# Attention and gated FFN on one core: scores in stages of eight blocks that cross units, values in one stage per unit, eight PSUM banks shared out anew, three load slots

## The chip, the core and the metric

The kernel runs on one core of a Trainium2 chip. The metric is the device time in microseconds (us) of one execution; of the kernel before, three runs gave a median of 1071.33 us (1071.3 to 1072.25).

## What is computed

Windowed causal attention with a linear bias over 8 batches of 8 heads (576 positions, head size 64), and then a gated FFN on all 4608 tokens (model width 512, hidden width 1536). All in fp32; q, k and the gate's weights are drawn several times wider than usual.

```python
scores = q @ k.transpose(0, 1, 3, 2) / sqrt(64)
mask = (rel >= 0) & (rel < 128)                       # rel = query position - key position
scores = where(mask, scores - slope[h] * abs(rel), -1e9)
attn = softmax(scores)                                # sum + 1e-9 in the denominator
x = (attn @ v) laid out as (4608, 512)
gate = 1 / (1 + exp(-(x @ w_gate)))
out = (gate * (x @ w_val)) @ w_out
```

## The kernel before, in words

**Attention** is worked in 32 *units*: one batch and a pair of heads each. The two heads' 1152 tokens are cut into 9 *blocks* of 128 queries. A block's queries see its own 128 keys and the 128 before them, so its scores are one matmul of 64 contraction rows into 256 columns (the first block of a unit: 128). Even blocks lie on the lower 64 rows of TensorE's array and odd ones on the upper 64, and two such matmuls run side by side. In the kernel before a unit's blocks go in three *score stages* of 3, 4 and 2 blocks (`group`, line 339), into the two banks `sp`; for the first four units every other stage goes into two of the FFN's banks instead. VectorE (DVE) then merges each bank's two halves (line 350), adds the bias and takes the row minimum (line 356, "the reduction"); ScalarE (ACT) takes the exponential with its sum (line 360); DVE makes the reciprocal; DVE or ACT scales the row (lines 368 and 369). TensorE transposes the group's blocks into the bank `tp` (line 373), ACT or DVE copies them out, and GpSimd spreads them into `pt` with the triangle masks (line 384). The *values* (line 409) are matmuls of 128 rows into 64 columns, one head on the lower and one on the upper half of the array's columns, side by side too. A unit has two value stages: output positions 0 to 320 and 320 to 576. The result is copied to `xt` and sent to DRAM (`xs`).

**The FFN** keeps fp32 accuracy with three fp32r products a matmul (high and low parts). Its first third of the hidden width (`w1`, tiles of 512 tokens, nine of them) runs among the attention: per tile 4 gate and 4 value projections of 12 matmuls each (line 454), each in one PSUM bank, and 4 output projections of 12 (line 492), 144 matmuls in all. After a value projection DVE multiplies by the gate in the bank (line 470), ACT casts the high part (line 173) and DVE subtracts for the low part (line 182); only then is the bank free. The other two thirds (`w2`, lines 584 to 615) run behind, with a scheme of seven products; they need the attention's SBUF, which is given back when the last unit is done, and weights that are split on DVE and ACT from then on.

**PSUM** has eight banks of 128 x 512: before, four (`mm0` to `mm3`) for the FFN, two for the scores, one for the transposes, one for the values.

**What sets the order.** Every piece of work is an `Op` with an engine, a cost and keys that it reads and writes. `Graph.order` is a list scheduler: it takes the op that can start first, ties by its due time `want` (FFN matmuls on TensorE come last), and the engines then get their instructions in that fixed order. One `add` is one piece: a whole score stage, a whole value stage, three FFN matmuls. Outside the first units every attention piece on TensorE is planned to start 1 us (`SLACK`) after its inputs. All DMAs go out on SP's queue.

Of the kernel before, what the change touches and what calls it, by code (L numbers as in the profile page):

```python
# [150 lines left out]
def attention_gated_ffn(ctx: ExitStack, tc: tile.TileContext, qd, kd, vd, wg, wv, wo, out):  # L151
# [88 lines left out]
    raws, mms, banks = [0], [0], [4]  # L240
# [64 lines left out]
    def load(u):  # L305
        want = u.when(-len(GROUPS))
        cuts = (0, 3, NBLK) if u.n == 0 else (0, NBLK)
        for h, (b0, b1) in enumerate(zip(cuts, cuts[1:])):
            sl, q0, q1 = slice(b0 * P, b1 * P), (b0 + 1) // 2, (b1 + 1) // 2
            keys = range(b0, b1)  # L310
            move(lambda sl=sl: kraw(u)[:, sl], lambda sl=sl: kd[u.b, u.p, :, sl], [], [("kr", u.s, i) for i in keys], want, 64 * (b1 - b0))
            move(lambda q0=q0, q1=q1: qraw(u)[:, q0:q1], lambda q0=q0, q1=q1: qd[u.b, u.p, :, q0:q1], [],
                 [("qr", u.s, i) for i in range(2 * q0, 2 * q1)], want, 64 * (q1 - q0))
        move(lambda: vraw(u), lambda: vd[u.b, u.p], [], [("vr", u.s)], want, 288)

    count = [0]

    def group(u, k):
        m = count[0]
        count[0] += 1  # L320
        blks = GROUPS[k]
        n = len(blks)
        want = u.when(k)
        slack = 0.0 if u.n < HEAD else SLACK
        early = u.n < EARLY and m % 2
        banks = [mm[r].rearrange("p (a q) -> p a q", a=2) for r in range(2)] if early else sp
        kbank = [("mm", r) if early else ("sp", r) for r in range(2)]
        kst, kpb, kb = ("st", m % 4), ("pb", m % 3), ("both", m % 2)
        st = lambda: T(att, f"st{m % 4}", [P, 12], F32)
        pb = lambda: T(att, f"pb{m % 3}", [P, 4, P], F32)  # L330
        both = lambda: T(att, f"both{m % 2}", [P, 4, P], F32)
        spot = {i: (i % 2, sum(j % 2 == i % 2 for j in blks[:a])) for a, i in enumerate(blks)}

        def scores():
            for i in blks:
                r, a = spot[i]
                lo = P if i == 0 else 0
                rows = slice(r * D, r * D + D)
                nc.tensor.matmul(banks[r][:, a, lo:], qraw(u)[rows, i // 2], kraw(u)[rows, (i - 1) * P + lo:(i + 1) * P],  # L339
                                 start=True, stop=True)  # L340
# [5 lines left out]
        for r in used:
            a = [spot[i][1] for i in blks if i % 2 == r and i]
            if a:
                a0, a1 = a[0], a[-1] + 1
                g.add("DVE", dve_cost((a1 - a0) * P, psum=True), lambda r=r, a0=a0, a1=a1: nc.vector.copy_predicated(  # L350
                    banks[r][:, a0:a1, P:], before[:, a0:a1], banks[r][:, a0:a1, 0:P]), ["before"], [kbank[r]], want)
            for e, i in enumerate(blks):
                if i % 2 == r:
                    mid = NBLK // 2
                    w = 0 if i == 0 else 1 if i < mid else min(4, i - mid + 2)
                    g.add("DVE", 0.21, lambda e=e, i=i, w=w: nc.vector.tensor_tensor_reduce(  # L356
                        pb()[:, e], banks[i % 2][:, spot[i][1], P:], relm[u.p][:, w], op0=ALU.add, op1=ALU.min,
                        scale=-0.125, scalar=3.0e38, accum_out=st()[:, e:e + 1]), [kbank[r]], [(kpb, e), (kst, e)], want)
# [370 lines left out]
```

## Time and profile before

| | |
|---|---|
| median of 3 runs | 1071.33 us (1071.3 to 1072.25) |
| profiled execution | 1071.71 us, span 1070.0 us, granted clock 0.997 |
| TensorE busy | 1059.2 us, 99% of the span |
| DVE, ACT, GpSimd busy | 694.1, 549.3 and 110.8 us |
| score matmuls (L339), as recorded | 576 records, 91 us |
| value matmuls (L409), as recorded | 832 records, 74.1 us |

[...] Recorded matmul durations overlap, so what TensorE needs for a piece is read from the distance between starts, not from the sum of the durations. The profiled execution is 1.71 us longer than its span and 0.38 us longer than the median.

### The profile page before, as it was taken

What the parts mean: (1) busy time and instruction counts of PE and PEld (TensorE: products, weight loads), DVE (VectorE), ACT (ScalarE), POOL (GpSimd) and SP (SyncE); (2) the same over time, 40 slices, a digit from 0 to 9 for tenths busy, and PEclk for the clock granted to TensorE, in tenths of its full rate; (3) what the DMA queues carried; (4) which work ended last, traced back from release to release, by engine and by line L of the source; (5) the groups of instructions that cost most, each with busy time, mean ns of one, the idle gap of its engine ahead of it and who ended that gap; (6) DMA issues with size and microseconds to landing.
All of it is one profiled execution on the core that took longest, in us unless ns stands there. A gap on an engine that the chain in (4) does not pass through costs nothing.

```text
span 1070.0 us, 17032 instructions
## 1 busy us (share of the span) xinstructions
PE 1059.2 (99%) x5918; PEld 894.3 (84%) x5918; DVE 694.1 (65%) x1958; ACT 549.3 (51%) x1503; POOL 110.8 (10%) x207
## 2 busy tenths in 40 slices
PE   8899999999999999999999999999999999999998
PEld 6577677777777778888999899998989989899997
DVE  7896656665655638863565675746999465675743
ACT  7997776576667745432443352433755234251431
POOL 2333222222222210000000000000000000000000
PEclk9899999999999999999999999999999999999999
DMA  7667546545364415441222415134353532415122
GB/s 244 224 216 237 157 149 188 167 147 161 115 194 167 129 62 188 157 132 65 99 87 91 138 40 177 51 127 137 101 165 108 161 98 80 146 32 177 51 69 98
DMA packets 74726, 142.66 MB, mean 133 GB/s; under 512 B 7312, under 2 KB 30224, under 8 KB 74640
## 3 DMA queue, kind: packets, MB, share of 16 engines
q1 hardware_dynamic: 74640, 141.58, 40.7%
q8 instruction: 46, 0.75, 0.3%
q14 instruction: 40, 0.33, 0.1%
HBM read 103.81 MB, written 37.75 MB: 132 GB/s over the span
## 4 chain that ended last, share of the span: by engine, by line
PE 95%; ACT 2%; DVE 1%; DMA 1%; issue 0%; SPq 0%; ACTq 0%; DVEq 0%
PE mm L584 33%; PE mm L492 27%; PE mm L454 19%; PE sp L339 7%; PE avp L409 6%; PE tp L373 3%; ACT pb L360 1%; DMA xr<-xs 1%; ACT pb L368 0%; DVE xlo L182 0%; DMA qr<-in_q_dram 0%; ACT both L173 0%; DVE pb L356 0%; DVE mm L350 0%; PE mm L339 0%
## 5 line engine op out<-in xcount | busy, mean ns | idle before, releaser
L584 PE MATMUL mm<-xc,w2s 128*128 128x384 f32 x2016 | 354.9, 335 | 0.0
L584 PEld LDWEIGHTS mm<-xc,w2s 128*128 128x128 f32 x2016 | 351.2, 188 | 2.3 <-ACT a L173 0.3
L492 PE MATMUL mm<-w2o,hh 128*128 128x512 f32 x576 | 177.7, 390 | 0.0
L360 ACT ACTIVATE pb<-pb,st 128x128 f32<-128x128 f32 x288 | 113.2, 396 | 42.6 <-DVE st L356 42.4
L384 POOL TENSOR_SCALAR_AFFINE_SELECT pt<-both 128x384 f32<-128x384 f32 (+2 forms) x192 | 98.9, 540 | 276.3 <-ACT both L173 220.5
L492 PEld LDWEIGHTS mm<-w2o,hh 128*128 128x128 f32 x576 | 107.8, 188 | 21.3
L492 PE MATMUL mm<-w2o,hl 128*128 128x512 f32 x288 | 112.4, 390 | 0.0
L595 ACT ACTIVATE sg<-mm 128x384 f32<-128x384 f32 x96 | 47.4, 494 | 115.5 <-PE mm L584 76.2
L173 ACT COPY a<-mm 128x384 f32<-128x384 f32 x48 | 23.1, 481 | 148.1 <-PE mm L584 145.2
L454 PE MATMUL mm<-xhi,w1g 128*128 128x512 f32 x288 | 93.7, 407 | 0.4 <-DVE st L356 0.4
L454 PE MATMUL mm<-xhi,w1v 128*128 128x512 f32 x288 | 93.1, 404 | 0.0
L492 PE MATMUL mm<-w1o,hh 128*128 128x512 f32 x288 | 93.1, 404 | 0.0
L350 DVE COPY_PREDICATED sp<-before,sp 128x128 f32<-128x128 int32 (+1 forms) x180 | 52.8, 333 | 53.0 <-PE sp L339 52.4
L339 PE MATMUL sp<-kr,qr 64*128 64x128 f32 (+1 forms) x540 | 84.8, 406 | 1.4 <-DMA qr<-in_q_dram 0.8
L409 PEld LDWEIGHTS avp<-pt,vr 128*64 128x64 f32 x832 | 58.4, 137 | 25.6 <-issue 12.0
L591 DVE TENSOR_TENSOR mm<-mm,a 128x384 f32<-128x384 f32 x48 | 27.0, 563 | 72.9 <-PE mm L584 72.9
L409 PE MATMUL avp<-pt,vr 128*64 128x64 f32 (+3 forms) x832 | 74.1, 310 | 0.0
L368 ACT ACTIVATE pb<-pb,st 128x128 f32<-128x128 f32 x169 | 60.5, 398 | 19.3 <-DVE st L365 18.2
L339 PEld LDWEIGHTS sp<-kr,qr 64*128 64x128 f32 x540 | 46.5, 189 | 26.3 <-issue 13.8
L356 DVE CUSTOM_DVE_ANT_0 pb<-sp,relm 128x128 f32<-128x128 f32 x270 | 64.1, 283 | 0.1
L497 DVE SCALAR_TENSOR_TENSOR ob<-mm,pi 128x512 f32<-128x512 f32 x72 | 48.3, 684 | 23.7 <-PE mm L492 14.2
L492 PEld LDWEIGHTS mm<-w1o,hh 128*128 128x128 f32 x288 | 51.0, 188 | 14.9 <-issue 6.5
(109 smaller groups left out, 1516.7 us busy)
## 6 DMA issues: line engine op xcount, KB each, us to landing
part<-ob SPq DMA_DIRECT2D x72, 256.0 KB, 3.1
pi<-part SPq DMA_DIRECT2D x72, 256.0 KB, 3.3
kr<-in_k_dram SPq DMA_DIRECT2D x31, 576.0 KB, 4.4
xr<-xs SPq DMA_DIRECT2D x18, 768.0 KB, 5.5
qr<-in_q_dram SPq DMA_DIRECT2D x31, 320.0 KB, 4.9
vr<-in_v_dram SPq DMA_DIRECT2D x32, 288.0 KB, 3.5
xs<-xt SPq DMA_DIRECT2D x32, 288.0 KB, 3.7
out_dram<-ob SPq DMA_DIRECT2D x36, 256.0 KB, 2.1
```

The lines of the kernel that those rows point to most:

```text
L339: nc.tensor.matmul(banks[r][:, a, lo:], qraw(u)[rows, i // 2], kraw(u)[rows, (i - 1) * P + lo:(i + 1) * P], start=True, stop=True)
L350: g.add("DVE", dve_cost((a1 - a0) * P, psum=True), lambda r=r, a0=a0, a1=a1: nc.vector.copy_predicated(banks[r][:, a0:a1, P:], before[:, a ...
L356: g.add("DVE", 0.21, lambda e=e, i=i, w=w: nc.vector.tensor_tensor_reduce(pb()[:, e], banks[i % 2][:, spot[i][1], P:], relm[u.p][:, w], op ...
L360: g.add("ACT", 0.39, lambda e=e: nc.scalar.activation(pb()[:, e], pb()[:, e], AF.Exp, bias=st()[:, e:e + 1], scale=-1.0, accum_out=st()[:, ...
L368: g.add("ACT", 0.3, lambda args=args: nc.scalar.mul(*args()), [(kst, 8)], [(kpb, e)], want, ways=[("DVE", 0.16, True, lambda args=args: nc ...
L384: nc.gpsimd.affine_select(pt(u)[:, f0:f0 + 2 * n - 1:2, :], both()[:, 0:n], [[0, n], step], cmp, 0.0, base=0, channel_multiplier=mult)
L409: nc.tensor.matmul(avp[e * D:(e + 1) * D, a - e * S - t0:b - e * S - t0], vraw(u)[:, c], seen, start=(k == 0), stop=(k == len(todo[e]) - 1 ...
L454: nc.tensor.matmul(mm[s], w.tile(kind, wi)[:, i, c * P:(c + 1) * P], x()[:, c, :], start=(k == 0 and c == 0), stop=(k == 2 and c == KC - 1))
L492: nc.tensor.matmul(mm[s], x()[:, i, ts], w.tile("o", wi)[:, i, :], start=(i == 0 and k == 0), stop=(i == n - 1 and k == 2))
L497: g.add("DVE", dve_cost(DM, psum=True), lambda: nc.vector.scalar_tensor_tensor(ob(), mm[s], 0.5, pi(), op0=ALU.mult, op1=ALU.add), [("mm", ...
L584: nc.tensor.matmul(mm[b][:, 0:N2], w.tile2(i, wp)[:, wk, c * P:(c + 1) * P], combo(k, xp)[:, c], start=(start and c == 0 and j == 0), stop ...
L595: g.add("ACT", act_cost(N2, psum=True), lambda: nc.scalar.activation(sg[h](), bk(b)(), AF.Tanh, scale=0.5), [("mm", b)], [("sg", h)], F)
```

## The change

A **score stage** now takes the next eight blocks of one running sequence over all units (the next four for the first 72 blocks, that is the first eight units), so that a stage can hold the end of one unit and the start of the next. The rows of the array alternate by place in the stage; on the host the blocks of q are laid out so that a block's parity follows the unit's. A stage of eight fills four banks with two blocks each, a stage of four two of them. The softmax and the transposes go by three blocks, always within a unit. The **values** of a unit are one stage: 512 output positions in one bank and the last 64 in the unused quarter of the transposes' bank. **PSUM** is one pool of eight banks: `mm0` and `mm1` for the FFN, `mm2` to `mm5` for scores, `mm6` for transposes and the last 64 positions, `mm7` for values; FFN tiles 7 and 8 and all that follows go round all eight. q, k and v have three **load slots** instead of two. The planner's numbers change with it: the first eight units have no wait and no release time (four before), the weights of the first third are due from 25 on in steps of 2 (20 in steps of 4), and GpSimd and DVE are taken more readily as second choice.

```diff
-HEAD = 4
-EARLY = 4
-GROUPS = ((0, 1, 2), (3, 4, 5, 6), (7, 8))
+HEAD = 8
+RUN = 8
+SOON = 8
+TRI = 3
+NSLOT = 3
...
-RAMP = 10.0
+RAMP = 15.0
...
-W0, WSTEP = 20.0, 4.0
-SP_COST, SWITCH = 0.45, 0.2
+W0, WSTEP = 25.0, 2.0
+SWITCH = 0.3
 WARM = 30.0
-YIELD = {"DVE": 0.2, "POOL": 0.2}
+YIELD = {"DVE": 0.1, "POOL": 0.0}
...
-    mm = [ps_m.tile([P, NB], F32, name=f"mm{i}") for i in range(4)]
-    sp = [ps_a.tile([P, 2, 2 * P], F32, name=f"sp{i}") for i in range(2)]
-    tp = ps_a.tile([P, 4, P], F32, name="tp")
-    avp = ps_a.tile([P, NB], F32, name="avp")
+    mm = [ps_m.tile([P, NB], F32, name=f"mm{i}") for i in range(8)]
+    sp = [t.rearrange("p (a q) -> p a q", a=2) for t in mm[2:6]]
+    tp, avp = mm[6].rearrange("p (a q) -> p a q", a=4), mm[7]
+    TP, AVP = ("mm", 6), ("mm", 7)
...
-    raws, mms, banks = [0], [0], [4]
+    raws, mms, banks = [0], [0], [2]
...
+    def scores(blks):
+
+        u0, i0 = blks[0]
+        want = u0.when(i0)
+        slack = 0.0 if u0.n < HEAD else SLACK
+        spot = [(k % 2, k // 2) for k in range(len(blks))]
+        half = len(blks) == RUN // 2 and stages[0] % 2
+        stages[0] += 1
+        bank_of = lambda r, a: r * (RUN // 4) + a // 2 + half
+
+        def matmuls():
+            for (u, i), (r, a) in zip(blks, spot):
                 lo = P if i == 0 else 0
                 rows = slice(r * D, r * D + D)
+                nc.tensor.matmul(sp[bank_of(r, a)][:, a % 2, lo:], qraw(u)[rows, i // 2],
+                                 kraw(u)[rows, (i - 1) * P + lo:(i + 1) * P], start=True, stop=True)
...
+    def values(u):
+        want = u.when(NBLK + 1)
         slack = 0.0 if u.n < HEAD else SLACK
-        t0, t1 = ((0, CUT), (CUT, S))[part_]
+        spots = ((0, NB, lambda: avp), (NB, S, lambda: tp[:, TRI, 0:S - NB]))
...
+        need = [("pt", u.s, i, own) for i in range(NBLK) for own in range(2)]
+        g.add("PE", 1.81 + 0.15 + SWITCH, matmuls, need + [("vr", u.l)], [AVP, TP], want, slack=slack)
...
+    stream = [(u, i) for u in units for i in range(NBLK)]
+    for n in range(NSLOT - 1):
+        load(units[n])
+    at = 0
     for u in units:
...
+        while at < (u.n + 1) * NBLK:
+            n = RUN // 2 if at < SOON * NBLK else RUN
+            scores(stream[at:at + n])
+            at += n
...
         if u.p == NPAIR - 1:
             while todo1 and (todo1[0] + 1) * NB <= (u.b + 1) * S:
+                banks[0] = 8 if todo1[0] >= LATE else 2
                 ffn(todo1.pop(0), w1)
```

The order of TensorE (PE) in the middle of the attention, before: the end of a three-matmul FFN piece, the second value stage of a unit (`avp`), its last score stage of two blocks (`sp`), and the FFN again.

```order
L492 MATMUL mm1_147<-w1o0_877,hl_819 128x512
L409 MATMUL avp_153<-pt0_243,vr0_164 64x64
L409 MATMUL avp_153<-pt0_243,vr0_164 64x128
L409 MATMUL avp_153<-pt0_243,vr0_164 64x192
L409 MATMUL avp_153<-pt0_243,vr0_164 64x256
L409 MATMUL avp_153<-pt0_243,vr0_164 64x192
L409 MATMUL avp_153<-pt0_243,vr0_164 64x128
L409 MATMUL avp_153<-pt0_243,vr0_164 64x64
L339 MATMUL sp1_151<-kr1_166,qr1_171 128x256
L339 MATMUL sp0_150<-kr1_166,qr1_171 128x256
L492 MATMUL mm2_148<-w1o0_877,hh_807 128x512
```

The order of PE in the middle of the attention, now (scores L341, transposes L390, FFN L469): FFN, a transposition, a stage of eight blocks that begins with the last block of one unit (`kr0`) and goes on into the next (`kr1`), and FFN.

```order
L469 MATMUL mm1_144<-xlo_406,w1v0_580 128x512
L390 MATMUL mm6_149<-ident_71,pb3_263 128x128 x3
L341 MATMUL mm2_145<-kr0_151,qr0_153 128x256
L341 MATMUL mm4_147<-kr1_166,qr1_168 128x128
L341 MATMUL mm2_145<-kr1_166,qr1_168 128x256
L341 MATMUL mm4_147<-kr1_166,qr1_168 128x256
L341 MATMUL mm3_146<-kr1_166,qr1_168 128x256
L341 MATMUL mm5_148<-kr1_166,qr1_168 128x256
L341 MATMUL mm3_146<-kr1_166,qr1_168 128x256
L341 MATMUL mm5_148<-kr1_166,qr1_168 128x256
L469 MATMUL mm0_143<-xhi_389,w1g0_414 128x512
```

Where there were a stage of two blocks and a partial value stage between FFN pieces, there is one stage of eight; the whole values of a unit (`mm7`, `mm6`) stand in one piece elsewhere. Counted over all of PE's order, the array passes from full use to halves and back 110 times each way before, and 57 times now; scores and values stand next to each other 47 times before and 15 times now.

The order of PE where the first FFN matmuls stand, before: transpositions, the first piece of a projection in `mm0`, and scores.

```order
L373 MATMUL tp_152<-ident_74,pb1_218 128x128 x4
L373 MATMUL tp_152<-ident_74,pb2_202 128x128 x2
L454 MATMUL mm0_146<-xhi_341,w1g0_374 128x512
L454 MATMUL mm0_146<-xhi_341,w1g1_381 128x512
L454 MATMUL mm0_146<-xlo_351,w1g0_374 128x512
L339 MATMUL sp0_150<-kr0_154,qr0_156 128x128
L339 MATMUL sp1_151<-kr0_154,qr0_156 128x256
L339 MATMUL sp0_150<-kr0_154,qr0_156 128x256
```

And now: the end of the values of the second unit, the first projection's first piece in `mm0` (FFN L469), a transposition, the second projection's first piece in `mm1`.

```order
L427 MATMUL mm7_150<-pt1_392,vr1_170 64x64
L427 MATMUL mm6_149<-pt1_392,vr1_170 64x64 x4
L469 MATMUL mm0_143<-xhi_389,w1g0_414 128x512
L469 MATMUL mm0_143<-xhi_389,w1g1_444 128x512
L469 MATMUL mm0_143<-xlo_406,w1g0_414 128x512
L390 MATMUL mm6_149<-ident_71,pb2_220 128x128 x3
L469 MATMUL mm1_144<-xhi_389,w1g0_414 128x512
L469 MATMUL mm1_144<-xhi_389,w1g1_444 128x512
L469 MATMUL mm1_144<-xlo_406,w1g0_414 128x512
L390 MATMUL mm6_149<-ident_71,pb3_263 128x128 x3
```

Before, 36 blocks' scores, two units' values and 27 transposed blocks stand ahead of the first FFN matmul; now 36 blocks, two units' values and 18 transposed blocks. From here on two FFN projections can be open at a time, four before.

The order of DVE over the start of a score stage in the middle of the attention, before: two merges of the bank's halves (L350) and three reductions (L356) with the reading of their minima, then a copy, the sums.

```order
L350 COPY_PREDICATED sp0_150<-before_81,sp0_150 128x128
L350 COPY_PREDICATED sp1_151<-before_81,sp1_151 128x128
L356 ISA pb0_181,st1_219<-sp0_150,relm3_89 128x128
L356 ISA st1_219 128x1
L356 ISA pb0_181,st1_219<-sp0_150,relm3_89 128x128
L356 ISA st1_219 128x1
L356 ISA pb0_181,st1_219<-sp1_151,relm3_89 128x128
L356 ISA st1_219 128x1
L174 COPY both0_240<-tp_152 128x256
```

And now: four merges (L354), and the reductions (L362) of eight blocks in three groups, with an FFN piece (L485) among them.

```order
L354 COPY_PREDICATED mm2_145<-before_78,mm2_145 128x128
L354 COPY_PREDICATED mm4_147<-before_78,mm4_147 128x2x128
L354 COPY_PREDICATED mm3_146<-before_78,mm3_146 128x2x128
L354 COPY_PREDICATED mm5_148<-before_78,mm5_148 128x2x128
L362 ISA pb0_192,st0_193<-mm2_145,relm0_83 128x128
L362 ISA st0_193 128x1
L485 SCALAR_TENSOR_TENSOR mm1_144<-sg1_737,mm1_144 128x512
L362 ISA pb0_192,st0_193<-mm4_147,relm0_83 128x128
L362 ISA st0_193 128x1
L362 ISA pb0_192,st0_193<-mm2_145,relm0_83 128x128
L362 ISA st0_193 128x1
L182 TENSOR_TENSOR hl_860<-mm1_144,hh_844 128x512
```

A stage's banks are free for the next stage when the last of its reductions has read them: after four, three or two reductions before, after eight now.

More of the change, by code (lines that the diff above doesn't have):

```diff
@@ L314, in load @@
[L314 to L336, printed above, removed]
+                 [("qr", u.l, i) for i in range(2 * q0, 2 * q1)], want, 64 * (q1 - q0))
@@ L348, in group @@
+        g.add("PE", cost + SWITCH, matmuls, [("qr", u.l, i) for u, i in blks] + [("kr", u.l, j) for u, i in blks for j in (i - 1, i) if j >= 0],
+              [("mm", 2 + b) for b in used], want, slack=slack, release=max(u.rel(i) for u, i in blks))
+        for b, on in sorted(used.items(), key=lambda kv: blks.index(kv[1][0][:2])):
+            a = [a for u, i, a in on if i]
             if a:
                 a0, a1 = a[0], a[-1] + 1
-                g.add("DVE", dve_cost((a1 - a0) * P, psum=True), lambda r=r, a0=a0, a1=a1: nc.vector.copy_predicated(
-                    banks[r][:, a0:a1, P:], before[:, a0:a1], banks[r][:, a0:a1, 0:P]), ["before"], [kbank[r]], want)
@@ L352, in group @@
[L352 to L358, printed above, removed]
@@ new lines, in probabilities @@
+    def probabilities(u, i0):
+        m, _, st, pb, kst, kpb = three_of(u, i0)
+        want = u.when(i0 + TRI)
+        slack = 0.0 if u.n < HEAD else SLACK
+        n, kb = TRI, ("both", m % 2)
+        both = lambda: T(att, f"both{m % 2}", [P, TRI, P], F32)
+        g.add("DVE", 0.07, lambda: nc.vector.tensor_scalar_add(st()[:, 6:9], st()[:, 3:6], 1.0e-9),
+              [(kst, 3 + e) for e in range(n)], [(kst, 6)], want)
+        g.add("DVE", 0.09, lambda: nc.vector.reciprocal(st()[:, 6:9], st()[:, 6:9]), [], [(kst, 6)], want)
+        for e in range(n):
+            args = lambda e=e: (pb()[:, e], pb()[:, e], st()[:, 6 + e:7 + e])
+            g.add("ACT", 0.3, lambda args=args: nc.scalar.mul(*args()), [(kst, 6)], [(kpb, e)], want,
@@ L382, in spread @@
             def spread(own=own, step=step, cmp=cmp, mult=mult):
[L383 to L384 removed]
+                f0 = 2 * i0 + own
+                nc.gpsimd.affine_select(pt(u)[:, f0:f0 + 2 * n - 1:2, :], both(), [[0, n], step], cmp, 0.0,
                                         base=0, channel_multiplier=mult)
[L387 removed]
@@ new lines, in matmuls @@
+        def matmuls():
+            for e, c, a, b, first, last, t0, to in runs:
+                seen = pt(u).rearrange("p s t -> p (s t)")[:, (c + 1) * P + a:(c + 1) * P + b]
+                nc.tensor.matmul(to()[e * D:(e + 1) * D, a - e * S - t0:b - e * S - t0], vraw(u)[:, c], seen,
+                                 start=first, stop=last, skip_group_check=True)
+        need = [("pt", u.s, i, own) for i in range(NBLK) for own in range(2)]
+        g.add("PE", 1.81 + 0.15 + SWITCH, matmuls, need + [("vr", u.l)], [AVP, TP], want, slack=slack)
@@ L653, in close @@
         pools["w2"] = ctx.enter_context(tc.tile_pool(name="wpool2", bufs=1))
-        ps_b = ctx.enter_context(tc.tile_pool(name="ps_b", bufs=1, space=PSUM))
-        mm.extend(ps_b.tile([P, NB], F32, name=f"mm{i}") for i in range(4, 8))
     touched = sorted({k for k in list(g.writer) if (k if isinstance(k, str) else k[0]) in
-                      ("kr", "qr", "vr", "pt", "sp", "tp", "avp", "xt", "both", "before")
+                      ("kr", "qr", "vr", "pt", "xt", "both", "before")
                       or (isinstance(k, tuple) and isinstance(k[0], tuple))}, key=str)
     g.add("PY", 0.0, close, [], touched + ["w2pool"], FIRST)
-    banks[0] = 8
     for f0 in range(FC1, NFC, FC1):
```

144 lines of the change are left out of this document (71 added, 73 removed).

## The prediction

> **What bounds the kernel now.** I read the page's busy shares and slices first, then the chain, then TensorE's waits.
>
> ```profile
> PE 1059.2 (99%) x5918; PEld 894.3 (84%) x5918; DVE 694.1 (65%) x1958; ACT 549.3 (51%) x1503; POOL 110.8 (10%) x207
> PE   8899999999999999999999999999999999999998
> PEclk9899999999999999999999999999999999999999
> PE 95%; ACT 2%; DVE 1%; DMA 1%; issue 0%; SPq 0%; ACTq 0%; DVEq 0%
> ```
>
> TensorE is busy everywhere, at full clock but for the start, and the chain that ends last is 95% its own. What does not shorten TensorE's own work, or the first tens of us, changes nothing. Its waits, the largest and the one for a load:
>
> ```profile
> PE tp L373 <- ACT both L173: 1.5, 2, 1.3
> PE sp L339 <- DMA qr<-in_q_dram: 0.8, 1, 0.8
> ```
>
> All of them fall into the first 37 us; none is an FFN matmul's wait for a PSUM bank. But busy is not streaming, so I looked at starts on TensorE's timeline in mid-attention (start, length, line, tile, records):
>
> ```profile
> 202.72 0.40 PE L454 MATMUL mm<-xlo,w1v 128*128 128x512 f32 x1
> 203.04 1.20 PE L409 MATMUL avp<-pt,vr 128*64 128x256 f32 x12
> 204.17 1.13 PE L339 MATMUL sp<-kr,qr 64*128 64x256 f32 x8
> 205.24 0.73 PE L454 MATMUL mm<-xhi,w1v 128*128 128x512 f32 x2
> 205.81 0.40 PE L454 MATMUL mm<-xlo,w1v 128*128 128x512 f32 x1
> ...
> 208.23 0.62 PE L454 MATMUL mm<-xhi,w1g 128*128 128x512 f32 x2
> 208.69 0.40 PE L454 MATMUL mm<-xlo,w1g 128*128 128x512 f32 x1
> 209.02 0.70 PE L339 MATMUL sp<-kr,qr 64*128 64x256 f32 x4
> 209.65 0.73 PE L454 MATMUL mm<-xhi,w1g 128*128 128x512 f32 x2
> 210.22 0.39 PE L454 MATMUL mm<-xlo,w1g 128*128 128x512 f32 x1
> 210.45 0.62 PE L454 MATMUL mm<-xhi,w1g 128*128 128x512 f32 x2
> 210.92 0.39 PE L454 MATMUL mm<-xlo,w1g 128*128 128x512 f32 x1
> 211.14 0.61 PE L454 MATMUL mm<-xhi,w1g 128*128 128x512 f32 x2
> ```
>
> Three FFN matmuls take 0.69 us (210.45 to 211.14), 0.23 each. A stage of four blocks lasts 0.43 us more than one of two (1.13 against 0.70): a side-by-side pair of 256 columns streams in 0.43. From 208.23 to 211.14 lie nine FFN matmuls (2.06) and one pair: 2.91 - 2.06 = 0.85, of which 0.43 streams. So entering and leaving the half-array form costs 0.42, **0.21 a change of form**. From 202.72 to 205.81 lie three FFN matmuls (0.69), a first value stage and a stage of four blocks: 2.40. The blocks stream 0.86, the values' longer half (192 + 256 + 128 = 576 columns) 0.97; 0.57 is left for three changes, 0.19 each, so the step from row halves to column halves costs like the others. I take 0.195. This time counts as busy, and nothing hides it.
>
> **The change, part by part.**
>
> *Streams: no change.* Scores before: the stage of three is bound by blocks 0 and 2 (0.65), then 0.86 and 0.43, 1.94 a unit, 62 us in all; now 288 blocks in pairs, 144 x 0.43 = 62. Values: 576 + 512 columns on the longer half before, 960 + 128 in the new split, 1088 both times. There are 96 transposing groups and 1296 FFN matmuls as before.
>
> *Changes of form.* Before 110 + 110 + 47 = 267, now 57 + 57 + 15 = 129. All 138 would be 26.9 us. But ahead of the first FFN matmul (22 before, 14 now) nothing is won, since there TensorE waits for softmax. That leaves 130, **25.4 us** at most.
>
> *The start.* How much of that counts depends on when TensorE, not DVE and ACT, sets the pace.
>
> ```profile
> 50.00:90.00 40.00, 40.00 (x271) 28.53 (x267) 36.45 (x141) 37.25 (x126) 14.68 (x24) 1.00 0.69 226
> 120.00:150.00 30.00, 30.00 (x196) 21.63 (x196) 17.05 (x92) 21.20 (x78) 6.97 (x14) 1.00 0.39 122
> L356 DVE CUSTOM_DVE_ANT_0 pb<-sp,relm x194: 259/284/292, 119.8 to 379.9; 128x128 f32<-128x128 f32 x194
> L465 ACT ACTIVATE sg<-mm 128x512 f32<-128x512 f32 x36 | 21.4, 595 | 26.0 <-PE mm L454 25.9
> 84.29 0.90 DVE L182 TENSOR_TENSOR w1o<-wbits,w1o 128x512 fp32r<-128x512 f32 x1
> 95.23 0.40 PE L492 MATMUL mm<-w1o,hl 128*128 128x512 f32 x1
> ```
>
> The first two rows are stretches (after the length: busy of PE, PEld, DVE, ACT, POOL). From 50 to 90 us DVE and ACT are 91% and 93% busy, splitting weights beside the attention; from 120 on, 57% and 71%. The last split weight of the first third is written at 84.29, behind 70 reductions in DVE's order. Now it stands behind 84, because the attention goes first and the weights are due later. In steady work 194 reductions take 260 us, 1.34 each, in which DVE and ACT work (17.05 + 21.20) / 30 x 1.34 = 1.71 us together. Part of it is the FFN's: a tile has 16 pieces on ACT (0.60, the L465 row) and 12 on DVE (0.69, below), 18 us, and by the order a unit takes 25 of a tile's 144 matmuls along, so 3.1 us a unit, 0.35 a block. A block alone is 1.36. Fourteen more are 19 us on two engines at 92%: 10.4 us, and the weights are ready at **95.5 us**. At that time the old order stands at 108 FFN matmuls, 79 blocks, 7.5 units' values (the row at 95.23); the new one at about 93, 88 and 7. So TensorE is ahead by 9 blocks (1.9 us) and behind by 15 matmuls (3.4) and half a unit's values (0.9): **2.4 us behind**. What was saved in changes until then went into waiting. From there 202 changes were left, now 92: 110 x 0.195 = **21.5 us** saved. Sum: 19.1.
>
> *Two banks for projections.* A value projection's bank is busy until DVE, ACT and DVE are through with it; a quick and a slow case:
>
> ```profile
> 87.18 0.40 PE L454 MATMUL mm<-xlo,w1v 128*128 128x512 f32 x1
> ...
> 87.61 0.70 DVE L470 SCALAR_TENSOR_TENSOR mm<-sg,mm 128x512 f32<-128x512 f32 x1
> 88.96 0.69 DVE L182 TENSOR_TENSOR hl<-mm,hh 128x512 fp32r<-128x512 f32 x1 [0.21 <-ACT hh L173]
> ...
> 442.10 0.39 PE L454 MATMUL mm<-xlo,w1v 128*128 128x512 f32 x1
> 443.57 0.68 DVE L470 SCALAR_TENSOR_TENSOR mm<-sg,mm 128x512 f32<-128x512 f32 x1
> 445.69 0.68 DVE L182 TENSOR_TENSOR hl<-mm,hh 128x512 fp32r<-128x512 f32 x1
> ```
>
> 87.58 to 89.65 is 2.07 us; 442.49 to 446.37 is 3.88, behind weight splitting. Four banks hid both; two leave the other projection's 12 matmuls, 12 x 0.23 = 2.74 us, plus what attention the planner puts between. The last values stand behind 915 FFN matmuls, 6.35 tiles, so some 25 such handovers fall under it. Bounds: none, or (3.88 - 2.74) x 25 = 28 us. Under the attention the loads are those of the 120 us row, near the quick case, so I take 1 us.
>
> *A stage of eight blocks* is free after four merges and eight reductions on DVE, two and four at most before:
>
> ```profile
> 82.20 0.72 DVE L350 COPY_PREDICATED sp<-before,sp 128x256 f32<-128x256 int32 x2
> 83.45 0.28 DVE L356 CUSTOM_DVE_ANT_0 pb<-sp,relm 128x128 f32<-128x128 f32 x1
> 83.66 0.29 DVE L356 CUSTOM_DVE_ANT_0 pb<-sp,relm 128x128 f32<-128x128 f32 x1
> ```
>
> Merges are about 0.33 apart, reductions 0.21: 3.0 us, some 5 with the sums, scalings and FFN pieces that DVE's order has among them. TensorE has 27 FFN matmuls and three transposing groups, over 6.5 us, between two such stages in the middle of the order. I cost it at nothing; if that cover fails by half a us in each of 27 stages it is 13 us.
>
> *Less cover behind the attention.* The second FFN's first weights are split when the last unit is done:
>
> ```profile
> L173 ACT CAST w2s<-wbits x2: 621/622/622, 399.1 to 416.5; 128x512 fp32r<-128x512 f32 x2
> L182 DVE TENSOR_TENSOR w2o<-wbits,w2o x4: 685/692/692, 437.0 to 456.3; 128x512 fp32r<-128x512 f32 x4
> ```
>
> That takes 58 us. 561 FFN matmuls (128 us) covered it, now 381 (87 us): still enough, nothing. The third load slot puts the third unit's three loads ahead of the first FFN weights on SP's queue:
>
> ```profile
> kr<-in_k_dram SPq DMA_DIRECT2D x31, 576.0 KB, 4.4
> ...
> 36.42 1.22 PE L454 MATMUL mm<-xhi,w1g 128*128 128x512 f32 x2 [0.39 <-DVE st L356]
> ```
>
> So those weights may come about 4 us later (one landing); they are wanted at the first FFN matmul, at 36.42, which waits for DVE, so nothing. Loads held TensorE once, for 0.8 us, at the start.
>
> *Sum:* 1071.7 - 21.5 + 2.4 + 1.0 = 1053.6 in the profiled execution's terms; the median stood 0.4 lower: **1053 us**, own range 1046 to 1060.
>
> **Rivals.**
>
> *The start is no limit* (0.14). If DVE and ACT keep up with TensorE from the first FFN matmul on, all 130 changes count: 1071.3 - 25.4 = 1046, 1044 at 0.21 a change. For it: TensorE was fully busy from 50 us on. Against: 91% and 93%.
>
> *Late stages or a longer start* (0.14). Stages of eight arrive half a us late, or the start loses 10 us more: 1060 to 1069. For it: all four score banks are taken at once. Against: the cover above.
>
> *Two banks stall TensorE* (0.14). At the slow case every handover costs 1.1 us, 28 in all: 1053 - 1 + 28 = 1080; it undoes the gain from 0.8 us a handover on, so of this chance 0.06 ends at no change and 0.08 slower. Waiting also costs clock: behind the first waits above the granted clock fell.
>
> ```profile
> 35.00:37.50 2.50, 1.77 (x5) 1.12 (x5) 1.25 (x12) 2.45 (x12) 1.97 (x4) 0.50 0.98 371
> 37.50:40.00 2.50, 2.50 (x11) 1.26 (x11) 1.65 (x6) 2.34 (x8) 0.00 (x0) 0.50 0.41 160
> ```
>
> The column before the DMA share is the clock: half speed for these 5 us, 2.5 lost. The same may be saved or lost at the new start, which is in my range. The Trainium skill ("TensorE: Matmul & The Clock Gate", A second HAM failure mode: psum-queue depth-cycling) says that a kernel cycling through PSUM banks can leave TensorE idle between groups so often that its clock keeps falling back. By that rule the two banks would end in this rival; the trace, with four banks and full clock from 42 us on, neither bears it out nor excludes it.
>
> **How the numbers follow.** Forecast 0.58, the three rivals 0.14 each. About 0.2%, 2 us, is what a measurement here can tell from no change. Faster: 0.58 + 0.14 + 0.14 = 0.86; same 0.06; slower 0.08. The range leaves out the slower cases and the best end: 1043 to 1070.
>
> **What would show it.** Right: the FFN's first third ends some 18 us earlier, TensorE without waits after about 95 us, score and value stages of 2.1 to 2.2 us between FFN pieces; DVE and ACT over 90% busy to about 95 us, with TensorE waiting for them there. Wrong: FFN matmuls of the first third waiting for DVE's `hl` or ACT's `sg` (two banks), scores waiting for reductions, a clock below 1.0 after 50 us, or the second FFN's start waiting for its weights. If the time is below 1046, the start was no limit; above 1060, look at the banks first.

## The result, and the profile after

| | before | after |
|---|---|---|
| median of four runs | 1071.32 us (1070.93 to 1072.25) | 1048.12 us (1047.18 to 1048.88) |
| ratio, with its 95% interval | | 0.9782 (0.9765 to 0.9799) |
| profiled execution, its span | 1071.71, 1070.0 us | 1047.56, 1045.9 us |
| granted clock | 0.997 | 0.999 |

The change makes the kernel 23.2 us faster. That is inside the predicted range and inside the forecast's own range, 4.9 us below the forecast of 1053 and 2.1 us above the rival in which the start is no limit.

The page of the kernel after: TensorE's share, its slices, its clock, and the chain that ended last.

```profile
PE 1034.8 (99%) x5940; PEld 905.1 (87%) x5940; DVE 700.9 (67%) x1986; ACT 523.8 (50%) x1417; POOL 112.8 (11%) x209
PE   8899999999999999999999999999999999999998
PEclk9999999999999999999999999999999999999999
PE 95%; DVE 2%; ACT 2%; DMA 0%; issue 0%; SPq 0%; ACTq 0%
```

TensorE is the bound as before, with 24.4 us less of busy time (1059.2 before) for the same streams. Its waits are still all short, but one is new:

```profile
PE mm L390 <- ACT xt L173: 2.1, 3, 1.2
...
PE mm L390 <- DVE xt L174: 1.3, 2, 0.9
...
```

The transposes (L390) now wait for `xt`, the copy of a unit's last 64 positions out of the bank that they share. No FFN matmul (L469, L507) is in the list. The stretches of the start, after first (length, then busy of PE, PEld, DVE, ACT and POOL, then the clock), show where these waits lie:

```profile
0.00:30.00 30.00, 26.95 (x197) 21.61 (x199) 25.14 (x133) 20.80 (x82) 8.22 (x20) 1.00 0.83 288
30.00:60.00 30.00, 26.14 (x208) 19.44 (x204) 27.81 (x125) 27.37 (x101) 9.57 (x18) 1.00 0.72 249
60.00:95.50 35.50, 35.50 (x239) 28.17 (x240) 34.97 (x137) 29.95 (x102) 11.12 (x18) 1.00 0.68 210
95.50:400.00 304.50, 304.50 (x1990) 245.69 (x1989) 178.92 (x881) 188.52 (x646) 70.61 (x140) 1.00 0.47 152
```

The kernel before, in the first two of these stretches:

```profile
0.00:30.00 30.00, 26.66 (x185) 19.84 (x185) 23.67 (x125) 22.53 (x85) 8.28 (x20) 1.00 0.73 246
30.00:60.00 30.00, 26.73 (x164) 18.10 (x165) 26.01 (x109) 28.05 (x99) 10.82 (x18) 0.89 0.67 224
```

TensorE is idle for 6.9 us in the first 60 us, 6.6 before, and then not again until its last matmul, although DVE is 99% busy from 60 to 95.5 us. The clock of 0.89, which cost 30 x 0.11 = 3.3 us before, is gone.

A stage's price can be read from starts in the middle of the attention (kernel after, TensorE's timeline: start, length, line, tile, records):

```profile
309.02 0.39 PE L469 MATMUL mm<-xlo,w1v 128*128 128x512 f32 x1
309.25 0.49 PE L390 MATMUL mm<-ident,pb 128*128 128x128 f32 x3
309.67 2.00 PE L341 MATMUL mm<-kr,qr 64*128 64x256 f32 x16
...
312.17 0.40 PE L469 MATMUL mm<-xlo,w1v 128*128 128x512 f32 x1
...
312.86 0.40 PE L469 MATMUL mm<-xlo,w1v 128*128 128x512 f32 x1
313.19 2.08 PE L427 MATMUL mm<-pt,vr 128*64 128x256 f32 x26
...
315.77 0.40 PE L469 MATMUL mm<-xlo,w1v 128*128 128x512 f32 x1
```

From 312.86 to 315.77 lie three FFN matmuls (0.69) and a whole unit's values: 2.91 - 0.69 = 2.22 us. Their longer half streams 1088 columns; at the prediction's 0.43 a pair of 256 that is 1.83, so 0.39 is two changes of form. It was 0.57 for three in the prediction's rows. The stage of eight, from 309.25 to 312.17, is dealt with at the first experiment.

### The profile page after: what moved, and what is told of

It reads as the page before. It is cut to its first block, busy times and chain, and to the rows that moved or that the text cites. A ratio compares the mean times of both kernels' runs of the same rounds, so it can differ in the third digit from the quotient of the medians.

```text
span 1045.9 us, 17036 instructions
## 1 busy us (share of the span) xinstructions
PE 1034.8 (99%) x5940; PEld 905.1 (87%) x5940; DVE 700.9 (67%) x1986; ACT 523.8 (50%) x1417; POOL 112.8 (11%) x209
## 4 chain that ended last, share of the span: by engine, by line
PE 95%; DVE 2%; ACT 2%; DMA 0%; issue 0%; SPq 0%; ACTq 0%
PE mm L599 34%; PE mm L507 29%; PE mm L469 19%; PE mm L341 6%; PE mm L427 5%; PE mm L390 3%; ACT pb L365 1%; DVE mm L354 1%; DMA kr<-in_k_dram 0%; DVE pb L362 0%; ACT pb L385 0%; ACT wbits L260 0%; PE mm L227 0%; ACT both L173 0%; DVE wbits L264 0%
## 5 line engine op out<-in xcount | busy, mean ns | idle before, releaser
L507 PE MATMUL mm<-w2o,hh 128*128 128x512 f32 x576 | 177.7, 390 | 0.0
L401 POOL TENSOR_SCALAR_AFFINE_SELECT pt<-both 128x384 f32<-128x384 f32 x192 | 99.4, 541 | 301.8 <-ACT both L173 280.2
L365 ACT ACTIVATE pb<-pb,st 128x128 f32<-128x128 f32 x288 | 113.0, 396 | 31.4 <-DVE st L362 31.3
L507 PEld LDWEIGHTS mm<-w2o,hh 128*128 128x128 f32 x576 | 107.8, 188 | 21.1
L507 PE MATMUL mm<-w2o,hl 128*128 128x512 f32 x288 | 112.4, 390 | 0.0
L469 PE MATMUL mm<-xhi,w1g 128*128 128x512 f32 x288 | 92.9, 404 | 0.0
L469 PE MATMUL mm<-xhi,w1v 128*128 128x512 f32 x288 | 92.5, 402 | 0.0
L507 PE MATMUL mm<-w1o,hh 128*128 128x512 f32 x288 | 92.4, 402 | 0.0
L362 DVE CUSTOM_DVE_ANT_0 pb<-mm,relm 128x128 f32<-128x128 f32 x288 | 70.1, 283 | 22.5 <-PE mm L390 22.3
L354 DVE COPY_PREDICATED mm<-before,mm 128x256 f32<-128x256 int32 (+1 forms) x144 | 50.5, 394 | 46.3 <-PE mm L341 45.3
L341 PE MATMUL mm<-kr,qr 64*128 64x256 f32 (+1 forms) x576 | 75.2, 382 | 1.3 <-DVE st L362 0.7
L173 ACT COPY both<-mm 128x384 f32<-128x384 f32 x95 | 45.2, 475 | 54.4 <-PE mm L390 51.0
L427 PEld LDWEIGHTS mm<-pt,vr 128*64 128x64 f32 x832 | 61.4, 137 | 11.9 <-issue 10.1
L341 PEld LDWEIGHTS mm<-kr,qr 64*128 64x128 f32 x576 | 53.6, 188 | 15.3 <-issue 5.8
L427 PE MATMUL mm<-pt,vr 128*64 128x256 f32 (+2 forms) x832 | 66.6, 306 | 0.0
L507 PEld LDWEIGHTS mm<-w2o,hl 128*128 128x128 f32 x288 | 54.1, 188 | 11.3
L512 DVE SCALAR_TENSOR_TENSOR ob<-mm,pi 128x512 f32<-128x512 f32 x72 | 48.3, 686 | 22.1 <-PE mm L507 12.5
```

Source lines behind the costliest of these rows:

```text
L173: g.add("ACT", act_cost(n, psum), lambda: nc.scalar.copy(out(), src()), reads, writes, want, release=release, ways=[("DVE", dve_cost(n, ps ...
L341: nc.tensor.matmul(sp[bank_of(r, a)][:, a % 2, lo:], qraw(u)[rows, i // 2], kraw(u)[rows, (i - 1) * P + lo:(i + 1) * P], start=True, stop= ...
L354: g.add("DVE", dve_cost((a1 - a0) * P, psum=True), lambda b=b, a0=a0, a1=a1: nc.vector.copy_predicated(sp[b][:, a0:a1, P:], before[:, a0:a ...
L362: g.add("DVE", 0.21, lambda: nc.vector.tensor_tensor_reduce(pb()[:, e], sp[b][:, a, P:], relm[u.p][:, w], op0=ALU.add, op1=ALU.min, scale= ...
L365: g.add("ACT", 0.39, lambda: nc.scalar.activation(pb()[:, e], pb()[:, e], AF.Exp, bias=st()[:, e:e + 1], scale=-1.0, accum_out=st()[:, 3 + ...
L401: nc.gpsimd.affine_select(pt(u)[:, f0:f0 + 2 * n - 1:2, :], both(), [[0, n], step], cmp, 0.0, base=0, channel_multiplier=mult)
```

## The experiments

Eight kernels ran, in two groups, each group beside its own runs of the kernel before (1071.58 and 1072.62 us). All but one are edits of the kernel after (1048.12); `before_new_numbers` is an edit of the kernel before. The kernel after ran in neither group, so a difference from its 1048.12 us also holds what the groups differ by: their kernels before differ by 1.0 us, and by up to 1.3 us from the 1071.32 of the result. Where it matters, the difference by ratios is given too: a run's ratio to its own group's kernel before, less the change's 0.9782, times 1071.3 us.

### What a change of form costs: `full_dummy` and `half_dummy`

Both put useless matmuls into the middle of every stage of eight, of which there are 27. The first puts one 128-row matmul there, so that the array goes back to its full form and again to halves. The second puts two 64-row ones of the same columns there, side by side, so that the form stays.

```diff
-            for (u, i), (r, a) in zip(blks, spot):
+            for k, ((u, i), (r, a)) in enumerate(zip(blks, spot)):
+                if k == RUN // 2:
+                    nc.tensor.matmul(sp[bank_of(0, 2)][:, 0, 0:P], ident, ident, start=True, stop=True)
```

In `half_dummy` the last line is

```diff
+                    for e in range(2):
+                        nc.tensor.matmul(sp[bank_of(e, 2)][:, 0, 0:P], ident[e * D:e * D + D],
+                                         ident[e * D:e * D + D], start=True, stop=True)
```

> The kernel after the change, with one added matmul of the identity (128 rows x 128 columns, fp32, full array) in the middle of each of the 27 score stages of eight blocks; it writes into a score bank just before a score matmul overwrites it. The plan is not told, so all other orders stay. Theory (what was saved is changes of form of the array, 0.20 us each): each stage has two more changes and 0.21 us more of streaming, 27 x (0.21 + 0.40) = 16.5 us, so 1064.6 us. Rival (what was saved is the number of pieces and their waits, the form is nothing): only the streaming, 27 x 0.21 = 5.7 us, 1053.8 us.

> As the full dummy, but the added work is two matmuls of 64 rows x 128 columns side by side, in the same form as the scores around them, so no change of form is added, and as much streaming. Theory: 27 x 0.21 = 5.7 us, so 1053.8 us, and 10.8 us less than the full dummy. Rival (number of pieces): the same as the full dummy within 2 us.

Measured: `full_dummy` 1063.62 us (1063.29 to 1065.29), `half_dummy` 1053.62 (1052.27 to 1056.28). The two kernels do the same added work and differ by 54 changes of form. The medians differ by 10.0 us, 0.185 us a change; with four runs each, spread over 2.0 and 4.0 us, that is 0.14 to 0.23 (95%). Single stages show it more sharply. In `full_dummy` (L340 is the useless matmul):

```profile
309.19 0.49 PE L392 MATMUL mm<-ident,pb 128*128 128x128 f32 x3
309.61 1.13 PE L343 MATMUL mm<-kr,qr 64*128 64x256 f32 x8
310.67 0.49 PE L340 MATMUL mm<-ident 128*128 128x128 f32 x2
...
312.72 0.40 PE L471 MATMUL mm<-xlo,w1g 128*128 128x512 f32 x1
```

In `half_dummy`:

```profile
314.48 0.49 PE L393 MATMUL mm<-ident,pb 128*128 128x128 f32 x3
314.90 0.92 PE L344 MATMUL mm<-kr,qr 64*128 64x256 f32 x7
...
317.63 0.39 PE L472 MATMUL mm<-xlo,w1v 128*128 128x512 f32 x1
```

From the transposes to the third FFN matmul behind them it takes 2.92 us in the kernel after (309.25 to 312.17 above), 3.15 in `half_dummy` and 3.53 in `full_dummy`. The pair of dummies adds 0.23, its own stream (half of a pair of 256 columns, 0.43 / 2); the full-array dummy adds 0.38 more, for two changes. Read in the same way at all 27 stages of eight, the pair of dummies adds 0.21 to 0.24, and `full_dummy` is 0.38 to 0.41 longer than `half_dummy`, 10.7 us together: **0.197 us a change**. The price on which the whole prediction rests is so shown; the prediction took 0.195.

The Trainium skill ("TensorEngine Tiling (Array Packing)", Key Properties) says that changing the tiling mode, not just the tile, drains TensorE. It gives no price. These runs show a cost at each change, as a drain would make one, and its size, 0.197 us; that the array drains they do not show.

### How much of it is the planner's numbers: `before_new_numbers` and `after_old_numbers`

The first is the kernel before with the planner's numbers of the change (the parts of `xhi` and `xlo` are still formed for the first four units only, and `SWITCH` stays as it was), the second the kernel after with those of before, the same lines the other way round.

```diff
-HEAD = 4
+HEAD = 8
-RAMP = 10.0
+RAMP = 15.0
-W0, WSTEP = 20.0, 4.0
+W0, WSTEP = 25.0, 2.0
-YIELD = {"DVE": 0.2, "POOL": 0.2}
+YIELD = {"DVE": 0.1, "POOL": 0.0}
```

> The kernel before, with the planner's numbers of the change alone (eight first units without wait and release, due times of the first weights, second choices taken more readily); stages, banks and slots as before. 270 changes of form against 267. Theory: the changes of form stay, only the start can differ, by the 3.4 us of half clock at 33 to 40 us and some waits there: 1066 to 1073 us. Rival (a good part of the gain came from the start and its numbers): 1063 us or less.

> The kernel after the change with the planner's old numbers (four first units without wait, weights due from 20 on in steps of 4, old second choices). 120 changes of form behind the first FFN matmul against 115. Theory: 1 us for five changes, and a start that was planned for other pieces, 0 to 8 us: 1049 to 1057 us. Rival (start and numbers): most of the gain is gone, 1060 us or more.

Measured: 1068.85 us (1067.50 to 1069.95) and 1054.99 (1053.99 to 1056.56). The numbers alone are worth 2.7 us in the old form (ratio 0.9971, 0.9960 to 0.9981), the new form alone 16.6 us (1071.58 to 1054.99; 0.9844, 0.9829 to 0.9858). With both the time is 1048.12, so the numbers are worth 6.9 us in the new form (6.6 by ratios). The stretches of `after_old_numbers` show where these are lost:

```profile
30.00:60.00 30.00, 27.27 (x184) 19.17 (x180) 26.02 (x110) 28.56 (x102) 10.25 (x18) 0.94 0.66 226
60.00:95.50 35.50, 34.22 (x223) 26.16 (x222) 29.66 (x105) 28.82 (x91) 8.53 (x14) 1.00 0.61 206
95.50:400.00 304.50, 301.61 (x1978) 241.66 (x1977) 183.73 (x897) 193.12 (x675) 70.73 (x142) 1.00 0.47 153
```

From 60 to 400 us TensorE is idle for 1.28 + 2.89 = 4.2 us, in the kernel after for none; the clock costs another 30 x 0.06 = 1.8. That is 6.0 of the 6.9. (Five more changes, 1.0 us, and 0.9 us less idle time in the first 60 us all but cancel.) So with the old numbers the start is a limit, and lasts past 95 us. With the new ones it hardly is.

### Two banks for projections: `two_value_stages`

The kernel after with the values of a unit in two stages again (0 to `CUT` = 320 and 320 to 576, both in `mm7`). The transposes' bank then holds no values, and a unit has two changes more. FFN projections still have two banks.

```diff
-                values(u)
+                values(u, 0)
+                values(u, 1)
...
-        spots = ((0, NB, lambda: avp), (NB, S, lambda: tp[:, TRI, 0:S - NB]))
+        t0, t1 = ((0, CUT), (CUT, S))[part_]
...
-        g.add("PE", 1.81 + 0.15 + SWITCH, matmuls, need + [("vr", u.l)], [AVP, TP], want, slack=slack)
+        g.add("PE", cost + SWITCH, matmuls, sorted(need) + [("vr", u.l)], [AVP], want, slack=slack)
```

> The kernel after the change with each unit's values in two stages again (positions 0 to 320 and 320 to 576, both in the values' bank, none in the transposes' bank). Its order has 167 changes of form behind the first FFN matmul, 52 more than the change, and the attention gets ahead: the last values stand behind 492 FFN matmuls, not 915, so 3.6 tiles run on two banks with no attention among them. Theory (changes of form, 0.19 us each as the dummies gave; two banks cost nothing): 1048.1 + 52 x 0.19 = 1058.0 us. Rival (two banks stall TensorE once nothing lies between the projections): 14 bare handovers of value projections at up to 1.1 us more, 1060 to 1073 us, with FFN matmuls (L469 of the change) waiting for DVE's low part.

Measured: 1054.31 us (1053.62 to 1055.73), below what either side had expected. Without the bank that transposes and values share, the planner ran the attention through much faster, the last values behind 492 FFN matmuls of its order, not 915. That makes it a harder test of the two banks than the change itself. Its stretch from 95.5 us on, and TensorE's two largest waits there:

```profile
95.50:400.00 304.50, 302.10 (x1948) 234.82 (x1945) 222.37 (x917) 192.45 (x648) 76.15 (x143) 1.00 0.53 173
```

```profile
PE mm L510 <- DVE hl L182: 1.1, 3, 0.6
PE mm L472 <- DVE hl L182: 0.6, 1, 0.6
```

With DVE 73% busy (59% after) FFN matmuls do wait for `hl`, four times, 1.7 us in all. Two of the four, 0.9 us, stand at output matmuls that read `hl` itself, so at most 0.8 us are waits for a bank. This is the rival's mechanism; even the 1.7 us are a sixteenth of the prediction's 28. In `after_old_numbers` they came to 1.3 us.

The theory had added 52 changes, 9.9 us; 6.2 were measured (5.4 by ratios). TensorE is busy longer in this kernel's start:

```profile
0.00:30.00 30.00, 27.82 (x203) 21.65 (x203) 25.87 (x139) 21.84 (x87) 9.77 (x22) 1.00 0.82 294
30.00:60.00 30.00, 29.06 (x222) 21.16 (x220) 28.89 (x137) 29.89 (x118) 10.95 (x20) 1.00 0.75 251
```

27.82 + 29.06 against 26.95 + 26.14 is 3.8 us. TensorE's waits for `xt` are 0.7 us here and 3.4 in the change. So the shared bank costs something at the start, where the theory had seen no cost. The sum does not close: 9.9 + 2.4 (idle from 95.5 on) - 3.8 would be 8.5, 2.3 above what was measured, and I have not found these 2.3 us.

### Stages of eight: `stages_of_four`

```diff
-SOON = 8
+SOON = 32
```

All stages hold four blocks, as those of the first eight units do in the change. Where 27 stages of eight stood there are 54 of four, and 48 more changes behind the first FFN matmul.

> The kernel after the change with score stages of four blocks throughout (two of the four score banks in turn). 163 changes of form behind the first FFN matmul, 48 more. Theory: 1048.1 + 48 x 0.19 = 1057.2 us. Rival (stages of eight come late because all four banks must be read first): stages of four win some of that back, 1053 us or less.

Measured: 1057.73 us (1057.24 to 1059.45), ratio 0.9865 (0.9848 to 0.9881): 9.6 us more than the change, 0.20 for each of the 48 (8.9 and 0.185 by ratios). A stage of eight gives back no part of what it saves, as far as these numbers resolve it: the prediction's cost of nothing holds, and the rival of late stages does not.

### The third load slot: `two_slots`

```diff
-NSLOT = 3
+NSLOT = 2
```

> The kernel after the change with two load slots for q, k and v instead of three. 125 changes of form behind the first FFN matmul, 10 more, since loads now wait for the unit before the last and the planner puts pieces apart. Theory: 1048.1 + 10 x 0.19 = 1050.0 us. Rival (the third slot is needed to have a unit's first blocks in time): TensorE waits for loads at each unit, 0.3 us x 24 = 7 us, 1057 us.

Measured: 1057.40 us (1056.01 to 1059.06), 9.3 us more than the change (8.2 by ratios). The rival had the time right, but not the place: TensorE waits for a load 0.3 us in all. Stretches of `two_slots`, the start and two pieces of it:

```profile
0.00:30.00 30.00, 26.34 (x188) 21.96 (x190) 24.05 (x116) 21.14 (x77) 7.65 (x18) 0.94 0.73 250
30.00:60.00 30.00, 25.89 (x177) 18.30 (x173) 26.09 (x112) 25.59 (x91) 9.77 (x16) 0.83 0.63 212
...
45.00:50.00 5.00, 4.01 (x16) 2.78 (x17) 3.78 (x17) 3.52 (x14) 2.06 (x4) 0.54 0.60 216
50.00:55.00 5.00, 5.00 (x19) 2.83 (x15) 2.65 (x16) 3.79 (x16) 0.99 (x2) 0.50 0.51 184
```

And its longest wait, on the timelines of TensorE and ACT:

```profile
45.36 0.87 PE L390 MATMUL mm<-ident,pb 128*128 128x128 f32 x3 [2.16 <-ACT xt L173]
...
42.07 2.15 ACT L385 ACTIVATE pb<-pb,st 128x128 f32<-128x128 f32 x7
...
44.62 0.69 ACT L173 COPY xt<-mm 128x512 f32<-128x512 f32 x2
```

The copy that frees the shared bank stands behind seven scalings and a weight's cast on ACT; the transposes wait 2.16 us for it. Then the clock is at half, also from 50 to 55 us, where TensorE is fully busy. Over the first 60 us the clock costs 30 x (0.06 + 0.17) = 6.9 us. Ten more changes of form behind the first FFN matmul are 2.0, and TensorE's idle time is 2.3 us longer (0.9 in the first 60 us, the rest up to 465 us). Together they are 11.2, where the spans of the profiled executions differ by 10.7. Eight more warm-up matmuls (84 records against 68) would add 1.7, so the sum closes to some 2 us only. The clock of the other three executions is 0.994 to 0.996, against 0.993 in this one, so that they lost less by it. Why two slots lead to another start can be read from SP's queue. The kernel after, where the third unit's loads go ahead of the first weights:

```profile
4.78 0.65 SPq L178 DMA_DIRECT2D kr<-in_k_dram  x1
...
7.32 1.05 SPq L178 DMA_DIRECT2D wraw<-in_moe_w_gate_dram  x2
```

And `two_slots`:

```profile
4.77 1.44 SPq L178 DMA_DIRECT2D wraw<-in_moe_w_gate_dram  x2
11.43 0.33 SPq L178 DMA_DIRECT2D kr<-in_k_dram  x1
```

With two slots the third unit's keys come 6.7 us later, behind the first weights, and the planner's order of the start is another. That this order is what makes the waits, and the waits what makes the half clock, is read from these rows, not tested by itself. A run with the order of three slots and two slots of memory was not tried.

### A start without the shared bank: `hybrid_start`

The first four units have two value stages, in `mm7` only; the other units are as in the change. The first weights are also due 5 us earlier, so this run makes two edits at once.

```diff
+HV = 4
...
-W0, WSTEP = 25.0, 2.0
+W0, WSTEP = 20.0, 2.0
...
-                values(u)
+                if u.n < HV:
+                    values2(u, 0)
+                    values2(u, 1)
+                else:
+                    values1(u)
```

> The kernel after the change, with the values of the first four units in two stages that leave the transposes' bank alone, and the first weights due from 20 on. 117 changes of form behind the first FFN matmul, 2 more. In the profile of the change the transposes wait 3.4 us in the start for the copy of the last 64 positions out of their bank. If that wait sets the start, this is 2 to 3 us faster than the change, 1045 to 1046 us; if another wait takes its place, 1048 us.

Measured: 1047.57 us (1047.06 to 1049.60), ratio to before 0.9771 (0.9753 to 0.9788): not to be told from the change (0.9782, 0.9765 to 0.9799). It is 0.6 us faster by medians and 1.2 by ratios, so the run does not exclude that a part of the 2 to 3 us was won. The waits for `xt` are nearly gone, and others have come (TensorE's waits, and the stretch up to 95.5 us):

```profile
...
PE mm L465 <- ACT xt L174: 0.4, 2, 0.3
PE mm L548 <- DVE w1o L183: 0.4, 1, 0.4
```

```profile
60.00:95.50 35.50, 34.84 (x234) 27.06 (x232) 32.00 (x129) 31.41 (x107) 14.18 (x22) 1.00 0.63 208
```

TensorE now waits for `w1o`, a split weight, which it did not in the change. TensorE's idle time in the first 60 us is 4.0 us, 6.9 in the change. Against this stand 0.66 us of waiting up to 95.5 and eight more changes of form in the trace (137 against 129), 1.6 us. That the shared bank's wait does not set the start alone is read from these rows; with two edits in one run it is not shown.

## Why the prediction was right, and where it was off

**The price of a change of form: right.** 0.195 was taken; 0.197 by the stages of `full_dummy` against `half_dummy` (0.185 by their medians), 0.185 to 0.20 by `stages_of_four`.

**The start: right in its date, wrong in its result.** The weights were forecast to be ready at 95.5 us. The row of the last of them, in the kernel after, begins at 93.9:

```profile
L182 DVE TENSOR_TENSOR w1o<-wbits,w1o x4: 681/692/906, 77.4 to 93.9; 128x512 fp32r<-128x512 f32 x4
```

The step that failed is "2.4 us behind". TensorE was to stand at 93 FFN matmuls, 88 blocks and 7 units' values at 95.5 us. Groups of records up to 95.5 us, before and then after (a block has two score records, a unit 26 of values; gate and value projections have 32 + 32 + 16 + 16 in both):

```profile
L339 PE MATMUL sp<-kr,qr 64*128 64x256 f32 (+1 forms) x122 | 20.6, 429 | 1.4 <-DMA qr<-in_q_dram 0.8 <-DVE st L356 0.5
L339 PE MATMUL mm<-kr,qr 64*128 64x256 f32 (+1 forms) x36 | 6.2, 434 | 1.6 <-DVE st L356 1.5
L492 PE MATMUL mm<-w1o,hh 128*128 128x512 f32 x8 | 2.8, 431 | 0.0
L492 PE MATMUL mm<-w1o,hl 128*128 128x512 f32 x4 | 1.6, 394 | 0.0
```

```profile
L341 PE MATMUL mm<-kr,qr 64*128 64x256 f32 (+1 forms) x176 | 25.3, 394 | 1.3 <-DVE st L362 0.7 <-DMA kr<-in_k_dram 0.5
L427 PE MATMUL mm<-pt,vr 128*64 128x256 f32 (+2 forms) x208 | 16.7, 306 | 0.0
L507 PE MATMUL mm<-w1o,hh 128*128 128x512 f32 x12 | 3.9, 408 | 0.0
L507 PE MATMUL mm<-w1o,hl 128*128 128x512 f32 x5 | 2.0, 395 | 0.0
```

It stood at 113, 88 and 8, against 108, 79 and 7.5 before: five FFN matmuls (1.1), nine blocks (1.9) and half a unit's values (0.9) **ahead, 3.9 us**. The blocks were right. I had then read TensorE's place from its order at the point where these 88 blocks' scores stand, but TensorE had gone on from there, through 20 more FFN matmuls and a unit's values, while DVE worked off the scores. The working took the weights of the first third as one thing that TensorE waits for until the last is ready. They become ready one by one, and TensorE needed none before it was there: it was full from 60 us on. It was not far from a limit: in `hybrid_start` it waited 0.66 us for them at 93 to 94 us.

**From there on: right.** 202 against 92 changes left were forecast, 21.5 us. Counted in the trace they are 201 against 89: 112, at 0.197 22.1 us. With 3.9 ahead that is 26.0; the spans differ by 24.1, and the 1.9 us between are not traced. In the profiled execution's terms the forecast was 1053.6, and 1047.56 was measured. Most of these 6.0 us is the sign of one term, "2.4 us behind" (6.3 us from there to 3.9 ahead); the 1.0 for two banks was not spent either, and changes saved 0.6 more; the 1.9 that the sum leaves over go the other way.

**The clock** was left in the range: "the same may be saved or lost". It was saved, 3.3 us, and is most of the 3.9 ahead. So of the 6.3 us by which the forecast's term was off, 3.3 are the clock, which the working had not forecast either way, and 3.0 are the working. That the clock was kept is not a property of the form: with the old numbers 1.8 us of it stay lost, in `two_slots` 6.9 are, and `half_dummy` lost 1.7 us behind nearly the same waits as the kernel after (last section). In this it was in part luck.

**Two banks:** taken at 1 us, bounds 0 and 28. No FFN matmul waited for a bank; under the harder load of `two_value_stages` FFN matmuls waited 1.7 us for `hl`, at most 0.8 of it for a bank. That a kernel which cycles through PSUM banks can keep losing its clock (the Trainium skill, "TensorE: Matmul & The Clock Gate", A second HAM failure mode: psum-queue depth-cycling) is not borne out here: the clock is 0.999.

**A stage of eight at nothing, less cover at nothing:** right, by `stages_of_four`, and by the waits after, in which no weight stands.

**The third load slot at nothing: wrong.** The prediction looked for its cost in SP's queue and at the first FFN matmul, and found none. Its worth was on the other side: without it the change would be 8 to 9 us slower, mostly through the clock in the profiled execution.

**What would show it.** Stages of 2.1 to 2.2 us: 2.22 for the values above, and 2.1 for the stage of eight (309.02 to 312.17 less three FFN matmuls is 2.46 with its three transposes, and three transposes alone between FFN pieces take 0.33). TensorE without waits after 95 us: from 60 on. DVE above 90% to 95 us: yes; ACT 84%; TensorE waiting for them there: no. First third 18 us earlier: its last matmul starts 25.1 us earlier (519.37 before, 494.27 after); in the kernel before second-third matmuls already run from 504.89 on, so that this overstates it.

**The rivals.** "The start is no limit" came near: its 1046 counts all 130 changes, and TensorE lost nothing behind 60 us. It did lose before: ahead of 95.5 us 26 changes fewer (66 before, 40 after, 5.1 us) and the clock (3.3) would be 8.4, and 3.9 arrived. Eleven more warm-up matmuls (68 records ahead of 95.5 us, 46 before) at 0.215, which stand in for idle time, are 2.4 of the gap, three more transposes 0.3, the idle time 0.3, and 1.5 are not traced. The other two rivals are excluded by the time.

**A reading that was off:** not all of the waits before fall into the first 37 us. One FFN matmul waited 0.45 us for `xlo` at 117 us; it changes nothing in the sum.

**Not tested by itself:** that FFN tiles 7 and 8 and what follows go round all eight banks.

## What to carry to other kernels

When TensorE is busy all the time, look at the starts around each switch between full-array and half-array matmuls: here 112 fewer switches of about 0.2 us were worth some 22 us that no wait, gap or utilisation figure shows. When an engine is 90% busy ahead of a deadline, do not conclude that the next engine waits for it: follow both engines' places to the same instant, with the waiting engine allowed to run on through whatever is ready. And test a side edit that seems to cost nothing by taking it away, since what it buys may lie in another stage, as the load slot's did.

## What the hardware showed that was not expected

Half clock was dearer than the wait ahead of it. In `two_slots` a wait of 2.16 us was followed by ten us at a granted clock near 0.5 (45 to 55), a loss of 4.8 us, and the clock stayed at 0.50 through 5 us in which TensorE was fully busy. But the length of a wait alone does not decide. In the kernel after the longest wait behind the very start was 1.17 us, and no clock was lost there; `half_dummy` has nearly the same wait, in both kernels one of 0.62 us follows, and in `half_dummy` the clock then fell. The wait in the kernel after, the wait in `half_dummy`, and `half_dummy`'s stretch behind it:

```profile
50.75 0.55 PE L390 MATMUL mm<-ident,pb 128*128 128x128 f32 x3 [1.17 <-ACT xt L173]
...
50.17 0.55 PE L393 MATMUL mm<-ident,pb 128*128 128x128 f32 x3 [1.15 <-ACT xt L173]
...
52.30:55.70 3.40, 3.40 (x14) 2.40 (x14) 1.25 (x12) 2.99 (x9) 1.71 (x4) 0.50 0.89 340
```

The times at half clock in the starts of these runs are 3.4 us (`half_dummy`, `after_old_numbers`, `before_new_numbers`, and once in `two_slots` behind a wait of 1.90), 6.8 (the kernel before) and 10.2 (`two_slots`, 45.4 to 55.6): once, twice and three times the same length.

The Trainium skill ("TensorE: Matmul & The Clock Gate", Part 1) has the gate at half after an idle window of about 3.4 us and at full again after a busy one; in `two_slots` the half clock came behind a shorter wait and lasted about three times as long. What sets its length, and whether a wait starts it, these runs do not show.

The price of a change is nearly the same in every direction, as far as these rows resolve it: 0.21 and 0.197 between the full array and row halves (the prediction's pair, the dummies), 0.195 between it and column halves (0.39 for two, above), 0.19 where row halves, column halves and the full array follow each other (0.57 for three). Only the first was tested by an experiment.
